# Rounding float64 weights on the chip: the last addition moved from VectorE to TensorE and to transfers

## The chip, the core and the metric

The kernel runs on one core of a Trainium2 chip. A core has five engines with a queue each: TensorE (PE, whose weight loads are shown as PEld), VectorE (DVE), ScalarE (ACT), GpSimd (POOL) and SyncE (SP). Each takes its instructions in the order in which they stand in its queue; an instruction that waits for another engine holds up all that stand behind it. Transfers (DMAs) are issued from the queues of SP, ACT and POOL and are done by 16 DMA engines. The metric is the time of one execution in microseconds on the device. Before the change it is 669.28 us, the median of three runs (668.96 to 669.71).

## The reference

Two blocks, one after the other: a gated linear attention over 768 steps for 4 batches of 8 heads with 48 channels, then a two-layer MLP with an ELU. The MLP's weights come in as float64.

```python
def _attn_ref(q, k, v, a_re, a_im):
    mag = np.sqrt(a_re * a_re + a_im * a_im)
    scale = np.minimum(mag, 0.999) / (mag + 1e-06)
    a_re_n, a_im_n = (a_re * scale, a_im * scale)
    for t in range(S):
        ar, ai = (a_re_n[:, :, t, :, None], a_im_n[:, :, t, :, None])
        new_re = ar * S_re - ai * S_im
        new_im = ar * S_im + ai * S_re
        kv = np.einsum('bhd,bhe->bhde', k[:, :, t], v[:, :, t])
        S_re, S_im = (new_re + kv, new_im)
        y[:, :, t] = np.einsum('bhd,bhde->bhe', q[:, :, t], S_re)

def _moe_ref(x, w_in, w_out):            # x: 3072 x 384, w_in: 384 x 2048, w_out: 2048 x 384
    h = x @ w_in
    g = np.where(h > 0.0, h, np.exp(np.minimum(h, 0.0)) - 1.0)
    return (g @ w_out).astype(np.float32)
```

## The kernel before

**Units.** The sequence is cut into chunks of 128 steps, and two batches go together: a unit `u` is one chunk of one pair of batches, 12 units in all (u = 0 and 1 are the first chunks of the two pairs). Each unit goes through the gates (`squares`, `joined`, `logarithms`, `powers`, `lengths`, `ratios`, `slopes`, `angles`, `decays`, `turns`, `waves`, `scaled`, `gated`), through the attention (`transposed`, `scores`, `states`, `values`, `seam`), and then through the MLP: eight pieces of `inner` (six matmuls of 128x256 against w_in, L1210) each with its `elu` (two ACT instructions, L1219 and L1220, and one on DVE, L1221, that reads the PSUM tile and so sets it free), and `project` (L1235 for the first units) against w_out. Later units (from u = 2 or 3) use forms of the two MLP products with fewer multiplications (`mult`, L1455; `product`, L1319), for which sums of the weights are made once (`summed_in`, `combined`).

**The weights.** Every weight comes as a pair of 32-bit words. A block is 128 partitions by 768 numbers; there are eight of w_in, `("in", m)`, and eight of w_out, `("out", m)`. `fetch` (L641) loads one as it is into a tile of raw words: into the tags g0 and g1 for the first four blocks of w_in, into one of two `w64` buffers for the others. `_rounded` (L36) makes from it two parts on DVE with four instructions: f from the high word (L40, L43), the power of two of f (L46), and p, the low word times that power (L50). A fifth, L655, adds p and f into the weight tile. f and p lie in the two buffers of the tag `wt`. `convert` issues one of these five instructions each time it is called, block after block.

**What sets the order.** The opening, up to the point where all weights are rounded and the first MLP is through, is a list written out by hand, `first`: each entry is a step, and its instructions go to the queues in the order of the list. Among the steps stand the `(convert,)` entries that thread the rounding through DVE's other work, `fetch` entries that put loads into SP's queue, and `(warm, n)`, n matmuls of the identity with itself whose result nobody reads (L1557). After the list follows a plan with due times, 16 slots to a unit, the same in both kernels.

**PSUM and buffers around the change.** `inner` takes its output from three buffers of the tag `mlp`; `outs()` gives two tiles y0 and y1 with one buffer each, which `values` and `project` use. w_out's tile is written for the first time when `("out", 0)` is rounded; before that nothing lies in it.

**Steps that the prediction names.** `joined` for u = 0 sums two tiles on PE by multiplying each with the identity (L720). `turned` (L832) does the sums of angles on PE (L837), takes them to turns on DVE (L842, L845), and for u = 0 and 1 makes the absolute value of the turns on DVE (L849). `angles` is ACT's arctan (L815), for which ACT loads a table. `ends` for u = 0 and 1 is 16 small matmuls (L946), a copy on DVE (`once`, L951), and one more matmul and copy. `state_sums` holds DVE's sums of the states (L1077, L1079, L1081), which wait for PE's state products (L1064).

Of the kernel before, what the change touches and what calls it, by code (L numbers as in the profile page):

```python
# [16 lines left out]
C = 128  # L17
# [14 lines left out]
WF = 2  # L32
# [473 lines left out]
def kernel(  # L506
# [110 lines left out]
    def weights_of(kind, m):  # L617

        if kind == "in":
            n = WF * DM // NI  # L620
            dst, cols = w_in[:, :, ts(m, n)], ts(m, 2 * n)
            tag = "g" + str(m // 2) if m < 4 else "w64"
            t = sb.tile([C, WF * DM, 2], U32, tag=tag, bufs=2, name="w64")
# [23 lines left out]
    def rounded(kind, m):  # L647

        w, dst = raw.pop((kind, m))
        f = sb.tile([C, WF * DM], U32, tag="wt", bufs=2, name="wf")  # L650
        p = sb.tile([C, WF * DM], U32, tag="wt", bufs=2, name="wp")
        yield from _rounded(nc, w, f, p)
        n = dst.shape[-1]
        f, p = (x.bitcast(FP32).rearrange("p (b n) -> p b n", n=n) for x in (f, p))
        nc.vector.tensor_tensor(out=dst, in0=p, in1=f, op=ALU.add)  # L655
        done.append((kind, m))
        yield True

# [173 lines left out]
    def turned(u, n):  # L832
# [13 lines left out]
        if u < 2:  # L846
            if n == 0:
                x["cs"] = new("cs", 1, [C, NB * H, 2, D])
            nc.vector.tensor_scalar(  # L849
                out=x["cs"][:, n * H : (n + 1) * H, 0].bitcast(U32),  # L850
                in0=x["z"][:, n].bitcast(U32), scalar1=0x7FFFFFFF, scalar2=None,
                op0=ALU.bitwise_and,
            )
# [108 lines left out]
    def waves(u, part=None):  # L962
# [5 lines left out]
        for n in range(0, NB, step):  # L968
# [6 lines left out]
            if u > 1:  # L975
# [602 lines left out]
    def gates_of(u, *at):  # L1578
# [8 lines left out]
        (joined, 0, 0), (squared, "ai", 1), (joined, 0, 1), (logarithms, 0, 0),  # L1587
        (logarithms, 0, 1), (fetch, "in", 1), (fetch, "in", 2), (ratios, 0, 0), (lengths, 0, 0),
        (warm, 2), (warm, 1), (lengths, 0, 1), (sums, 1), *2 * [(convert,)],
        (table, "exp_and_others"), (ratios, 0, 1), (powers, 0, 0), (powers, 0, 1), (warm, 2),  # L1590
        (sums, 0), (warm, 1), (angles, 0, 0), (angles, 0, 1), (summed, 0), (summed, 1),
        (decayed, 0, 0), (turned, 0, 0), (decayed, 0, 1), (turned, 0, 1), (waves, 0, 0),
        (waves, 0, 1), (begun, 1), (warm, 1), (scaled, 0, "q", 0), (ends, 0), (scaled, 0, "k", 0),
        (scaled, 0, "k", 1), (scaled, 0, "q", 1), (warm, 1), (gated, 0, 0), (warm, 1), (noted, 0),
        (table, "natural_log"), (warm, 2), (gated, 0, 1), (warm, 2), *3 * [(convert,)],
        (transposed, 0, "k", 0), (transposed, 0, "q", 1), (carry_on, 0), (transposed, 0, "q", 0),
        *4 * [(convert,)], (scores, 0, 0), (transposed, 0, "k", 1), (scores, 0, 1), (load_a, 1),
        (squares, 1), (joined, 1), (fetch, "in", 3), (logarithms, 1), (states, 0, 0),
        (values, 0, 0), (powers, 1), (convert,), (states, 0, 1), (lengths, 1), (load_qk, 1),
        (convert,), (ratios, 1), (values, 0, 1), (seam, 0), (warm, 2), (warm, 2), (decays, 1),  # L1600
        (load_a, 2), (warm, 1), (inner, 0, 0), *2 * [(convert,)], (noted, 1), (scaled, 1),
        (warm, 4), (convert,), (load_v, 1), (slopes, 1), (ends, 1), *3 * [(convert,)],
        (inner, 0, 2), (elu, 0, 0), (convert,), (fetch, "in", 4), (angles, 1), (turns, 1),
        (waves, 1), (gated, 1, 0), (inner, 0, 4), (gated, 1, 1), (transposed, 1, "q", 0),
        (transposed, 1, "k", 0), (convert,), (scores, 1, 0), (load_v, 2), (convert,),
        (fetch, "in", 5), *2 * [(convert,)], (transposed, 1, "k", 1), (states, 1, 0), (convert,),
# [161 lines left out]
```

## Time and profile before

| | us |
|---|---|
| median of three runs | 669.28 (668.96 to 669.71) |
| the profiled execution | 669.23 |
| its span, first to last instruction | 667.1 |
| PE busy in the span | 639.6 (96%) |
| DVE busy | 503.6 (75%) |
| ACT busy | 419.2 (63%) |
| POOL busy | 154.4 (23%) |
| rounding on DVE: 16 x L40, L43, L46, L50, L655 | 8.9 + 15.3 + 8.9 + 15.3 + 15.2 |
| granted TensorE clock, mean | 0.993 |

The profile is of one execution. Its parts: busy time of each engine; the span in 40 slices of 16.7 us with the busy share of each engine in tenths; groups of instructions by line, with their tile names as out<-in, count, busy time and mean; and on request the instructions of an engine in order of time, where a bracket shows how long the engine had been idle before and what ended that. A matmul in fp32 shows as two records. The ends of matmuls are modelled, so records that lie behind one another can overlap by a tenth or two of a microsecond. Tile names leave out the numbers of buffers; `ee`, `g` and `mlp` are the MLP's, `wf` and `wp` are f and p, `n`, `cs`, `qg`, `kg`, `S` belong to the gates and the attention.

### The profile page before, as it was taken

To read this page: it belongs to the slowest core of one execution; us is meant where nothing else is said; L and a number is where in the kernel's file an instruction comes from. 1 tells how busy PE (TensorE), PEld (TensorE's weight loads), DVE (VectorE), ACT (ScalarE), POOL (GpSimd) and SP (SyncE) were. 2 spreads that over 40 slices of the span, in tenths; PEclk is the share of its full clock that TensorE was granted. 3 is DMA by queue.
4 is the path that set the end of the run, shared out by engine and by line. 5 is a ranking of instruction groups with operands and counts; after the bars stand their busy time and mean duration, and the time that the engine had idled before them with its cause. 6 is when DMAs were issued, how large, how long until landed. Compare 5 with 4: busy or idle time off the path is not lost.

```text
span 667.1 us, 17231 instructions
## 1 busy us (share of the span) xinstructions
PE 639.6 (96%) x7236; PEld 579.6 (87%) x7236; DVE 503.6 (75%) x801; ACT 419.2 (63%) x684; POOL 154.4 (23%) x200
## 2 busy tenths in 40 slices
PE   8899899999999899999999999999999999999995
PEld 6777786576898798998998998999999999999995
DVE  5889999968777788678678768768768768765481
ACT  6885455874846567667677677677677577471250
POOL 2000000112124303503503503503603602402000
PEclk9799999999999999999999999999999999999999
DMA  9986645630900632452451451451551551212100
GB/s 166 189 142 105 148 149 167 112 72 20 154 3 15 115 56 62 81 106 57 86 106 53 90 104 48 97 104 44 100 104 44 102 104 43 54 32 61 34 2 29
DMA packets 151443, 56.12 MB, mean 84 GB/s; under 512 B 129684, under 2 KB 143164, under 8 KB 151356
## 3 DMA queue, kind: packets, MB, share of 16 engines
q1 hardware_dynamic: 147616, 53.58, 38.8%
q0 software_dynamic: 3520, 1.20, 1.5%
q8 instruction: 59, 0.97, 0.6%
q14 instruction: 28, 0.23, 0.1%
q10 hardware_dynamic: 220, 0.14, 0.1%
HBM read 48.91 MB, written 4.80 MB: 81 GB/s over the span
## 4 chain that ended last, share of the span: by engine, by line
PE 44%; DVE 10%; ACT 8%; issue 3%; DMA 1%; SPq 0%; ACTq 0%; DVEq 0%
PE mlp L1319 18%; PE mlp L1455 10%; PE y L1455 5%; DVE g L1471 3%; PE w L1023 3%; DVE g L1480 3%; PE y L1109 2%; ACT ee L1477 2%; ACT ee L1476 2%; PE w L1064 2%; PE w L837 2%; DVE g L1297 1%; ACT L735 1%; DVE n L772 1%; ACT n L746 1%
## 5 line engine op out<-in xcount | busy, mean ns | idle before, releaser
L1319 PE MATMUL mlp<-w_out,g 128*128 128x192 f32 x640 | 111.8, 328 | 1.0 <-DVE ee L1331 1.0
L1319 PEld LDWEIGHTS mlp<-w_out,g 128*128 128x128 f32 x640 | 104.2, 190 | 4.4 <-DVE ee L1331 1.6
L1081 POOL TENSOR_TENSOR S<-S,T 128x384 f32<-128x384 f32 x36 | 30.9, 857 | 175.5 <-DVE S L1079 175.5
L1210 PE MATMUL mlp<-x,w_in 128*128 128x256 f32 x288 | 65.1, 381 | 3.0 <-DVE g L1221 2.6
L1210 PEld LDWEIGHTS mlp<-x,w_in 128*128 128x128 f32 x288 | 53.8, 190 | 11.7 <-DVE g L1221 3.1
L1471 DVE TENSOR_TENSOR g<-g,mlp 128x512 f32<-128x512 f32 x45 | 30.7, 682 | 40.1 <-ACT qt L1024 28.7
L1297 DVE TENSOR_TENSOR g<-g 128x512 f32<-128x512 f32 x80 | 54.4, 695 | 5.0 <-PE mlp L1319 3.8
L1455 PE MATMUL mlp<-x,w_in 128*128 128x128 f32 x424 | 56.2, 275 | 0.4 <-DVE o L1344 0.4
L1480 DVE SCALAR_TENSOR_TENSOR g<-ee,g 128x512 f32<-128x512 f32 x63 | 47.6, 755 | 11.1 <-ACT ee L1477 11.0
L1319 PE MATMUL mlp<-w,g 128*128 128x192 f32 x320 | 54.5, 329 | 0.0
L1319 PEld LDWEIGHTS mlp<-w,g 128*128 128x128 f32 x320 | 51.8, 190 | 0.6
L1455 PEld LDWEIGHTS mlp<-x,w_in 128*128 128x128 f32 x424 | 51.6, 192 | 0.8 <-DVE o L1344 0.6
L1476 ACT ACTIVATE ee<-g 128x512 f32<-128x512 f32 x63 | 39.5, 627 | 17.2 <-DVE g L1471 16.7
L1190 POOL DMA_DIRECT2D x<-y x62 | 29.8, 488 | 87.2 <-ACT y L1126 37.3
L1468 ACT COPY g<-mlp 128x512 f32<-128x512 f32 x36 | 21.1, 586 | 44.0 <-PE mlp L1455 43.7
L1477 ACT ACTIVATE ee<-ee 128x512 f32<-128x512 f32 x72 | 45.4, 631 | 2.3
L1024 ACT COPY qt<-w 128x512 f32<-128x512 f32 x48 | 25.8, 589 | 15.5 <-PE w L1023 15.4
L973 ACT ACTIVATE cs<-n 128x768 f32<-128x768 f32 (+1 forms) x14 | 10.5, 751 | 38.0 <-DVE n L845 37.9
L904 ACT ACTIVATE n<-w 64x384 f32<-64x384 f32 (+1 forms) x60 | 28.1, 486 | 8.9 <-PE w L889 8.3
L1455 PE MATMUL mlp<-x,g 128*128 128x128 f32 x224 | 29.7, 275 | 1.2 <-DVE o L1344 1.2
L1219 ACT ACTIVATE ee<-mlp 128x512 f32<-128x512 f32 x24 | 14.3, 595 | 25.6 <-PE mlp L1210 17.2
L1455 PE MATMUL y<-x,w_in 128*128 128x128 f32 x216 | 29.0, 277 | 1.4 <-ACT g L1468 1.4
(222 smaller groups left out, 1434.8 us busy)
## 6 DMA issues: line engine op xcount, KB each, us to landing
w<-in_moe_w_out_dram SPq DMA_DIRECT2D x8, 768.0 KB
g<-in_moe_w_in_dram SPq DMA_DIRECT2D x24, 256.0 KB
g<-in_moe_w_out_dram SPq DMA_DIRECT2D x24, 256.0 KB
w<-in_moe_w_in_dram SPq DMA_DIRECT2D x16, 288.0 KB
vn<-in_v_dram SPq DMA_DIRECT2D x24, 192.0 KB
ar<-in_a_re_dram SPq DMA_DIRECT2D x22, 192.0 KB
ai<-in_a_im_dram SPq DMA_DIRECT2D x22, 192.0 KB
q<-in_q_dram SPq DMA_DIRECT2D x22, 192.0 KB
```

The source lines that it names most:

```text
L904: nc.scalar.activation(out=flat(x[key][to, n : n + 1]), in_=t[of], func=AF.Exp, scale=sign)
L1024: nc.scalar.copy(out=o[:, h0 : h0 + 4], in_=t)
L1081: eng.tensor_tensor(out=new_s, in0=new_s, in1=wide, op=ALU.mult)
L1190: eng.dma_start(out=x["x"][ds(j * HP + D, G), i], in_=x["y"][ds(j * HP + i * G, G)])
L1210: nc.tensor.matmul(t[:, e], lhsT=w_in[:, i, ts(f + e, C)], rhs=x["x"][:, i], start=(i == 0), stop=(i == NI - 1),)
L1297: nc.vector.tensor_tensor(out=S_of(u, k, h), in0=a, in1=b, op=op)
L1319: nc.tensor.matmul(to, lhsT=a[:, m], rhs=b[:, m], start=(first and h == 0 and m == 0), stop=False, skip_group_check=True,)
L1455: nc.tensor.matmul(x["c" + c][:, ts(m, C)], lhsT=a[:, m], rhs=x["mix"][p], start=(p == BANKS[c][0] and m == 0), stop=False, skip_group_che ...
L1471: nc.vector.tensor_tensor(out=part(u, to), in0=part(u, a), in1=part(u, b), op=op)
L1476: nc.scalar.activation(out=e, in_=part(u, of), func=AF.Relu, scale=-1.0)
L1477: nc.scalar.activation(out=e, in_=e, func=AF.Exp, scale=-1.0)
L1480: nc.vector.scalar_tensor_tensor(out=part(u, to), in0=nat[u]["e", to], scalar=-1.0, in1=part(u, of), op0=ALU.add, op1=ALU.max,)
```

## The change

Four things are changed.

1. `rounded` no longer ends with L655 for all blocks. For blocks 1 to 5 of w_in (`by_matmul`) f and p are left in a part of w_out's tile, and a new step `added(m)` multiplies both with the identity on PE, one after the other into the same PSUM tile (512 columns into y0, 256 into y1), from where two ACT copies bring the sums into w_in. For all blocks of w_out, f is made in w_out itself and p is added to it by a transfer from POOL's queue that accumulates. Blocks 0, 6 and 7 of w_in keep the addition on DVE.
2. The raw words of blocks 4 and 5 of w_in go into a part of w_out's tile too, not into `w64`.
3. The absolute value in `turned` for u = 1 moves to ACT, into `waves`.
4. The list `first` is new from `seam(0)` on: the `added` steps are put in, seven `warm` matmuls are left out, several `fetch`, `inner` and `elu` steps stand elsewhere, and there are fewer `convert` entries.

```diff
@@ weights_of
-            tag = "g" + str(m // 2) if m < 4 else "w64"
-            t = sb.tile([C, WF * DM, 2], U32, tag=tag, bufs=2, name="w64")
+            if m in (4, 5):
+                t = w_flat[:, ts(m - 4, 2 * WF * DM)].rearrange("p (n two) -> p n two", two=2)
+            else:
+                tag = "g" + str(m // 2) if m < 4 else "w64"
+                t = sb.tile([C, WF * DM, 2], U32, tag=tag, bufs=2, name="w64")
@@ rounded
-        f = sb.tile([C, WF * DM], U32, tag="wt", bufs=2, name="wf")
-        p = sb.tile([C, WF * DM], U32, tag="wt", bufs=2, name="wp")
-        yield from _rounded(nc, w, f, p)
-        n = dst.shape[-1]
-        f, p = (x.bitcast(FP32).rearrange("p (b n) -> p b n", n=n) for x in (f, p))
-        nc.vector.tensor_tensor(out=dst, in0=p, in1=f, op=ALU.add)
+        if kind == "out":
+            f = dst.bitcast(U32).rearrange("p f n -> p (f n)")
+            p = sb.tile([C, WF * DM], U32, tag="wt", bufs=2, name="wp")
+        elif by_matmul(m):
+            f, p = (w_flat[:, ts(4 + m % 2 * 2 + n, WF * DM)] for n in range(2))
+        else:
+            f = sb.tile([C, WF * DM], U32, tag="wt", bufs=2, name="wf")
+            p = sb.tile([C, WF * DM], U32, tag="wt", bufs=2, name="wp")
+        each = _rounded(nc, w, f, p)
+        for _ in range(3):
+            yield next(each)
+        next(each)
+        f, p = f.bitcast(FP32), p.bitcast(FP32)
+        if kind == "out":
+            nc.gpsimd.dma_start(
+                out=dst.rearrange("p f n -> p (f n)"), in_=p, accum_op=ALU.add
+            )
+        elif by_matmul(m):
+            parted[m] = f, p, dst
+            yield True
+            return
+        else:
+            yield True
+            f, p = (x.rearrange("p (b n) -> p b n", n=dst.shape[-1]) for x in (f, p))
+            nc.vector.tensor_tensor(out=dst, in0=p, in1=f, op=ALU.add)
         done.append((kind, m))
         yield True
+    w_flat = w_out.bitcast(U32).rearrange("p f n -> p (f n)")
+    def by_matmul(m):
+        return 0 < m < 6
+    def added(m):
+        f, p, dst = parted.pop(m)
+        n = dst.shape[-1]
+        for t, (i, k) in zip(outs(), ((0, 2), (2, 1))):
+            for x in (f, p):
+                nc.tensor.matmul(
+                    t[:, 0 : k * n], lhsT=ident, rhs=x[:, ds(i * n, k * n)], start=(x is f),
+                    stop=(x is p),
+                )
+            nc.scalar.copy(
+                out=dst[:, ds(i, k)], in_=t[:, 0 : k * n].rearrange("p (i n) -> p i n", n=n)
+            )
+        done.append(("in", m))
@@ turned
+        if u < 1:
             nc.vector.tensor_scalar(
                 out=x["cs"][:, n * H : (n + 1) * H, 0].bitcast(U32),
@@ waves
-            if u > 1:
+            if u > 0:
                 nc.scalar.activation(out=cos, in_=z, func=AF.Abs)
```

The list from `seam(0)` to the first projection, before:

```python
(seam, 0), (warm, 2), (warm, 2), (decays, 1), (load_a, 2), (warm, 1), (inner, 0, 0),
*2 * [(convert,)], (noted, 1), (scaled, 1), (warm, 4), (convert,), (load_v, 1), (slopes, 1),
(ends, 1), *3 * [(convert,)], (inner, 0, 2), (elu, 0, 0), (convert,), (fetch, "in", 4),
(angles, 1), (turns, 1), (waves, 1), (gated, 1, 0), (inner, 0, 4), (gated, 1, 1),
(transposed, 1, "q", 0), (transposed, 1, "k", 0), (convert,), (scores, 1, 0), (load_v, 2),
(convert,), (fetch, "in", 5), *2 * [(convert,)], (transposed, 1, "k", 1), (states, 1, 0),
(convert,), (inner, 0, 6), (fetch, "in", 6), (elu, 0, 2), *4 * [(convert,)],
(transposed, 1, "q", 1), (scores, 1, 1), (fetch, "in", 7), (values, 1, 0), (states, 1, 1),
(values, 1, 1), (convert,), (seam, 1), *4 * [(convert,)], (inner, 0, 8), (inner, 0, 10),
(elu, 0, 4), *2 * [(convert,)], (elu, 0, 6), (elu, 0, 8), (fetch, "out", 0), (warm, 2),
(inner, 1, 0), (convert,), (inner, 0, 12), (convert,), (inner, 1, 2), *3 * [(convert,)],
(inner, 1, 4), (fetch, "out", 1), (fetch, "out", 2), (fetch, "out", 3), (elu, 0, 10), (convert,),
(inner, 0, 14), (elu, 1, 0), *3 * [(convert,)], (elu, 0, 12), (fetch, "out", 4),
...
(project, 0, 0, 0, 4),
```

and after:

```python
(seam, 0), (fetch, "in", 4), (warm, 2), (warm, 2), (decays, 1), (added, 1), (inner, 0, 0),
*2 * [(convert,)], (noted, 1), (scaled, 1), (inner, 0, 2), (fetch, "in", 5), (convert,),
(load_v, 1), (slopes, 1), (ends, 1), (added, 2), (convert,), (elu, 0, 0), (angles, 1),
(turns, 1), (convert,), (waves, 1), (convert,), (load_a, 2), (fetch, "in", 6),
(inner, 0, 4), (gated, 1, 0), (added, 3), (gated, 1, 1), (transposed, 1, "q", 0),
(transposed, 1, "k", 0), (convert,), (elu, 0, 2), (scores, 1, 0), (inner, 0, 6),
(load_v, 2), (convert,), (fetch, "in", 7), (convert,), (transposed, 1, "k", 1),
(states, 1, 0), (convert,), (elu, 0, 4), (added, 4), (convert,), (transposed, 1, "q", 1),
(scores, 1, 1), (convert,), (inner, 0, 8), (values, 1, 0), (states, 1, 1), (convert,),
(elu, 0, 6), (values, 1, 1), (convert,), (seam, 1), (added, 5), *2 * [(convert,)],
(fetch, "out", 0), (inner, 0, 10), (elu, 0, 8), *2 * [(convert,)], (inner, 1, 0),
(convert,), (elu, 0, 10), (convert,), (inner, 0, 12), (convert,), (inner, 1, 2),
(elu, 1, 0), *2 * [(convert,)], (fetch, "out", 1), (fetch, "out", 2), (inner, 1, 4),
(elu, 0, 12), (convert,), (inner, 0, 14), (elu, 1, 2), (fetch, "out", 3), *3 * [(convert,)],
(fetch, "out", 4), *2 * [(convert,)], (inner, 1, 6), *2 * [(convert,)], (fetch, "out", 5),
...
(project, 0, 0, 0, 4),
```

A step that puts work on several engines puts it into each queue at its place in the list: `(added, 2)` stands ahead of `(elu, 0, 0)` and `(angles, 1)` on ACT as it stands ahead of `(turns, 1)` on PE. The order of the later steps of the list is the same but for the number of `convert` entries between them.

## The prediction

> **What bounds the kernel now.** I read first the busy tenths over 40 slices, then the busy time by stage, then the PE queue's order of time, and last the ACT queue at the place where the change cuts in. The first two rows show that after the opening only PE is full; in the opening DVE is full too.
>
> ```profile
> PE   8899899999999899999999999999999999999995
> ...
> DVE  5889999968777788678678768768768768765481
> ```
>
> By stage (columns: stage, its length, then busy us and count of PE, PEld, DVE, ACT, POOL, the granted clock, the DMA share and GB/s):
>
> ```profile
> 20.00:41.70 21.70, 19.09 (x279) 16.88 (x279) 19.69 (x29) 16.94 (x33) 0.97 (x2) 0.85 1.01 157
> 41.70:79.08 37.38, 32.56 (x443) 27.47 (x443) 34.69 (x52) 21.53 (x42) 1.92 (x4) 1.00 0.75 133
> 79.08:103.98 24.90, 23.48 (x111) 20.34 (x109) 24.35 (x35) 12.18 (x20) 0.00 (x0) 1.00 0.47 157
> 103.98:137.00 33.02, 32.94 (x171) 19.95 (x172) 31.28 (x39) 25.60 (x33) 2.38 (x3) 1.00 0.54 121
> 137.00:216.00 79.00, 78.49 (x911) 65.20 (x911) 56.30 (x79) 49.86 (x86) 20.54 (x26) 1.00 0.30 56
> ```
>
> DVE is 93 to 98% busy from 41.7 to 137 us and that is what the change takes from. But PE is 87% busy already from 41.7 to 79 and from 79 on it has almost no idle left. Whether that PE time is real work is the main question, because the ends of matmuls are modelled. The PE queue answers it:
>
> ```profile
> 47.79 2.86 PE L1210 MATMUL mlp<-x,w_in 128*128 128x256 f32 x12
> 50.48 1.45 PE L837 MATMUL w<-n,sum_turns 128*128 128x384 f32 x4
> ...
> 70.43 2.86 PE L1210 MATMUL mlp<-x,w_in 128*128 128x256 f32 x12
> 75.94 2.86 PE L1210 MATMUL mlp<-x,w_in 128*128 128x256 f32 x12 [2.65 <-DVE g L1221]
> 78.63 0.61 PE L1557 MATMUL mlp<-ident 128*128 128x128 f32 x4
> 79.08 23.48 PE L1210 MATMUL mlp<-x,w_in 128*128 128x256 f32 x108
> 103.98 2.85 PE L1235 MATMUL mlp<-w_out,g 128*128 128x384 f32 x8 [1.42 <-DVE g L1221]
> ```
>
> One `inner` (12 records) takes 2.69 us alone (47.79 to 50.48) and 23.48/9 = 2.61 us in the row of nine; three of them from 164.1 to 172 us, where DVE has idle time, take 7.93/3 = 2.64. So the row of nine runs at PE's own pace, and DVE's fullness beside it costs PE nothing but the two bracketed waits. The waits of PE between 41 and 109 us are 2.65, 1.42, 0.92, 0.37, 0.36, 0.32, 0.28 and 0.24: 6.6 us together. That is all that relief of DVE can give back up to 109 us.
>
> **The change part by part.** *Taken from DVE:* the final add (L655, mean 0.955 us) of five w_in blocks and eight w_out blocks, 13 x 0.955 = 12.4, and two `cs` masks of u = 1 (L849, 0.36 each), 0.7: 13.1 us off DVE. On the path this is worth at most the 6.6 us above.
>
> *Added to PE:* each `added(m)` sends f and p through the identity, 2 x (512 + 256) = 1536 columns in fp32. The trace has the same operation, identity times a 128x384 fp32 tile, at `joined`: four matmuls, so 1536 columns,
>
> ```profile
> 6.74 2.75 PE L720 MATMUL w<-n,ident 128*128 128x384 f32 x8
> ```
>
> and they take 2.59 us to the next instruction and 2.75 with its tail; 2.65 is taken. Five of them are 13.2 us, on an engine with 6.6 us of gaps to put them in. Seven `warm` matmuls go (0.25 each, four fill 38.67 to 39.66): -1.7. If the new order were perfect, PE would end later by 13.2 - 1.7 - 6.6 = 4.9 us. This is the floor: 669.3 + 4.9 = 674.2.
>
> *Added to ACT:* two copies for each `added`, about 0.59 (128x512, L1024) and 0.37 (between the 0.32 of a 128x192 and the 0.48 of a 128x384 copy): 4.8 us in all, and two `Abs` of 0.5 (as L973 at 128x384, 0.52). ACT is 58% busy from 41.7 to 79, so the sum is covered; what costs is where they stand. ACT's queue in the kernel before reads here:
>
> ```profile
> 44.80 0.60 ACT L1219 ACTIVATE ee<-mlp 128x512 f32<-128x512 f32 x1 [0.29 <-PE mlp L1210]
> 45.42 0.63 ACT L1220 ACTIVATE ee<-ee 128x512 f32<-128x512 f32 x1
> 46.07 1.28 ACT L815 ACT_TABLE_LOAD   x1
> 47.37 0.84 ACT L815 ACTIVATE n<-n 128x768 f32<-128x768 f32 x1
> ```
>
> *The new order, walked with these durations.* Nothing differs on PE up to 41.0 us. Then PE has `added(1)` to 43.65, `inner(0,0)` to 46.3, `inner(0,2)` to 48.9, the matmuls of `ends(1)` to 51.1 (2.2, as from 45.58 to 47.79 before), `added(2)` to 53.75, and then `turns(1)`, which needs ACT's arctan. ACT's queue now holds the copies of `added(2)` ahead of `elu(0,0)`, the table load and the arctan: 53.75 + 0.4 + 1.25 + 1.28 + 0.85 = 57.55. So PE stands 3.9 us with `inner(0,4)` behind the waiting matmul, DVE's `once` has stood from 46.5 to 50.5, and the chain of u = 1 (turns, waves, gated) is 7.2 us late. DVE then does turns, the end of block 3 (62.4) and `gated` (65.9). On PE: turns to 58.95, `inner(0,4)` to 61.6, `added(3)` to 64.2, transposes to 66.0, 0.5 for ACT's copies, scores to 67.7, `inner(0,6)` to 70.3, transposes and states to 72.3. `added(4)` needs p of block 4. On DVE this stands behind `elu(0,2)` (its exp after a table load: 69.5), the mask, and the state sums, which wait for PE's states at 72.3: 74.9. PE waits 1.75 and is done at 76.7. In the same manner p of block 5 stands behind the state sums of n = 1 and is ready at 87.6: `added(5)` runs to 89.4 with 1.45 of waiting, and after 0.4 for ACT's copy `inner(0,10)` ends at 92.4. Before, it ended at 78.6. With a tail of some 0.2 after each wait (70.43 to 73.29 is 2.86 for 2.62) that is 14 to 15 us late; 13.2 of it is the added matmuls, the removed gaps and the new ones (8.3) nearly cancel.
>
> *After that* come ten `inner` and one projection, 30.6 us before (78.63 to 109.25). DVE rounds w_out in the same stretch. A block is now 0.6 + 0.99 + 0.6 + 0.99 = 3.2 us plus the `elu` between, but its load is issued when the second last block is done. Before it had 6.1 us for that (88.2 to 94.3) and DVE never waited: a load takes 6.1 us or less. At 6.1, loads hold DVE up for 1 to 1.5 us a block, and the `elu` behind give PE waits of about 1.0, 0.5 and 2.0 us where it had 1.42 and two `warm` before (0.5): +1.6. At 4.5 us there is no such wait: -1.5. I take the middle, 0.
>
> *The accumulating transfers* (8, issued by POOL, 384 KB each) are in no row. POOL is idle from 73 to 130 us, an issue costs 0.5 to 0.95 (L1190, L957). Per block, p must be added before its buffer is written again two blocks on; the walk leaves 7.5 us. From below: a 16 KB POOL transfer lands in 1.7 us. From above: 384 KB read twice and written once is less than twice a w_out load of 768 KB, so with the load beside it 6.1 + 6.1 us, and about 13 with the issue. I take 6 to 7 (nearest to the large load), which is covered; projections need block m some 5 to 15 us after its add. At 13 the cover is gone and DVE comes late for `lengths(2)` and `turns(2)`.
>
> [...]
>
> *From 109 us on* the queues are as before and PE is full (78.49 of 79.00 to 216), so the delay is carried to the end. *Sum:* +14 to +15 at the end of the opening. The profiled execution took 669.23 (span 667.1 and 2.1 around it), the median is 669.28: 669.3 + 14.7 = 684.
>
> **The rivals.** *A, well packed, 675 to 678:* my chain of waits is too pessimistic, PE's new gaps are 0 to 4 us in place of 8.3. For it: single waits rest on sums of 0.1 us. Against: the arctan stands behind four ACT steps that cannot begin before `added(2)` ends. *B, the accumulating transfers bind, 688 to 695:* a two-block cycle of 13 + 1.55 us is 7.3 a block where the walk has 4.6; six blocks later DVE is 16 us late, less some 5 of cover. For it: DMA share is already 0.5 there and each block now moves twice the bytes. Decides from about 8 us a transfer. *C, the other side, 661:* the opening is DVE's. If what is shown as busy PE were waiting for DVE's buffers, the added matmuls would slip into it and the change would give the 6.6 us and 1.7 of `warm`: 669.3 - 8.3 = 661. It decides from 4.9 us of hidden waiting in PE's rows from 41 to 137. For it: DVE has no gap in that stretch. Against: 2.61, 2.64 and 2.69 us for an `inner` at any load of DVE. *D:* the 3.6 us of PE idle from 216 to 250 vanish as well; these waits (for `o`, and for a load queued behind the output) move along with PE, so D is only a part of A.
>
> **How the numbers follow.** The walk 0.62, A 0.20, B 0.14, C 0.04. A measurement here tells 0.2% (1.3 us) from no change. A, B and the walk all lie above +4.9, so faster 0.03, same 0.02 (parts of C and of A with D), slower 0.95. The range reaches from the floor of A to the middle of B: 675 to 692.
>
> **What would show it.** Right: L655's group falls from 16 to 3; five identity groups of about 2.7 us on PE; a PE wait of about 4 us for the arctan before the sums of angles of u = 1, and shorter ones at `added(4)` and `added(5)`, both for DVE; `inner(0,10)` ending near 92; DVE with idle time between 46 and 90. For B: DVE's L46 of the w_out blocks waiting for a DMA. Wrong: an `inner` clearly shorter than 2.6 us, the identity sums well under 2.6 us, or first projections before 110 us.

## The result, and the profile after

The changed kernel takes 692.98 us (median of four runs, 689.36 to 699.17) against 669.50 (four runs, 668.96 to 669.71): a ratio of 1.0362, 95% interval 1.0272 to 1.0452. It is slower, as forecast, but by 23.5 us where the forecast had 14.7, and the median is 1 us above the range (two of the four runs, 689.36 and 689.63, lie inside it). The profiled execution took 696.32 (span 694.6), so it is one of the longer ones.

Busy tenths of PE and DVE, the granted clock of PE and the DMA share, in 40 slices of 17.4 us, from the page of the changed kernel:

```profile
PE   8797899898999979999999999999999999999996
...
DVE  5764468785767787867858858858858858856481
...
PEclk9988999999999999999999999999999999999999
DMA  9979216893092053244343443451560560211100
```

DVE's row of nines (slices 4 to 8 before) is gone, but PE now has sevens in slices 2 and 4, its clock shows an 8 twice, and the DMA share is at 8 and 9 in slices 8 and 9, where it was at 6 and 3. By stage of the changed kernel (columns as in the prediction); the boundaries are the last `warm`, the end of inner(0,10), the first projection, and the first transposes of u = 2:

```profile
20.00:42.60 22.60, 18.17 (x270) 16.28 (x270) 16.59 (x25) 15.90 (x30) 0.09 (x1) 0.80 0.93 150
42.60:99.10 56.50, 48.67 (x479) 35.95 (x479) 30.11 (x46) 27.55 (x54) 2.80 (x6) 0.94 0.56 88
99.10:126.27 27.17, 24.34 (x110) 20.13 (x108) 23.49 (x33) 12.53 (x20) 3.00 (x4) 1.00 0.68 184
126.27:166.25 39.98, 36.48 (x176) 21.62 (x177) 29.35 (x37) 27.73 (x35) 8.90 (x10) 0.96 0.77 165
```

The first projection begins at 126.27 where it began at 103.98 (+22.3), the transposes of u = 2 at 166.25 where they began at 138.77 (+27.5). The span grew by the same 27.5 (667.1 to 694.6): nothing is lost or won behind 166 us. In the last row PE is busy for 36.5 of 40.0 us where it had no gap before, and the DMA share is 0.77 in it. The PE queue of the changed kernel shows the places (start, duration, line, operation; in brackets the idle time before it and what ended that):

```profile
35.29 0.65 PE L1153 MATMUL y<-qt,S 128*48 128x64 f32 x16 [2.47 <-DVE S L1121]
35.88 3.65 PE L1108 MATMUL mlp<-vn,kg 64*128 64x48 f32 x32
...
44.36 2.74 PE L693 MATMUL y<-w_out,ident 128*128 128x512 f32 x8
46.94 5.34 PE L1254 MATMUL mlp<-x,w_in 128*128 128x256 f32 x24
...
61.05 2.93 PE L880 MATMUL w<-n,sum_turns 128*128 128x384 f32 x4 [3.78 <-ACT n L858]
63.77 4.15 PE L1254 MATMUL mlp<-x,w_in 128*128 128x256 f32 x12
...
81.49 1.99 PE L693 MATMUL y<-w_out,ident 128*128 128x512 f32 x6 [1.64 <-DVE w_out L50]
...
94.67 1.99 PE L693 MATMUL y<-w_out,ident 128*128 128x512 f32 x6 [0.87 <-DVE w_out L50]
96.50 21.23 PE L1254 MATMUL mlp<-x,w_in 128*128 128x256 f32 x96
...
126.27 2.85 PE L1279 MATMUL mlp<-w_out,g 128*128 128x384 f32 x8 [2.06 <-DVE g L1265]
...
142.80 0.88 PE L933 MATMUL w<-n,sum_logs 64*64 64x384 f32 x8 [0.77 <-DVE n L815]
...
160.79 1.15 PE L1108 MATMUL w<-vn,kg 64*64 64x48 f32 x64 [2.73 <-DVE kg L1047]
161.87 4.54 PE L1279 MATMUL y<-w_out,g 128*128 128x384 f32 x8
```

Two things are to be seen. An `added` takes what was forecast (44.36 to 46.94, 2.58 us, with 2.65 taken), and the waits for the arctan (3.78, forecast 3.9), before `added(4)` (1.64, forecast 1.75) and before `added(5)` (0.53 and 0.87, forecast 1.45) are there. But the work *behind* three of the waits takes longer than its kind: the 32 state products at 35.88 take 3.65 us (1.99 in the kernel before), the `inner` at 63.77 4.15 (2.75), the four projection steps at 161.87 4.54 (2.85). The granted clock in these stretches is 0.66, 0.66 and 0.76:

```profile
34.00:44.00 10.00, 8.71 (x107) 7.92 (x108) 7.10 (x11) 6.02 (x14) 0.97 (x2) 0.66 0.66 102
58.00:68.00 10.00, 6.96 (x17) 4.99 (x18) 5.72 (x9) 7.21 (x11) 0.49 (x1) 0.66 1.05 152
...
160.00:167.00 7.00, 6.21 (x79) 4.08 (x80) 6.02 (x7) 5.33 (x9) 2.30 (x2) 0.76 0.49 96
```

The kernel before has one such fall, from 19.7 to 26.5 us, and then none until its last 3 us. The last wait, 2.73 us for kg, is followed back through the queues of ACT and DVE in the changed kernel:

```profile
152.53 0.84 ACT L752 ACTIVATE n<-ar 128x768 f32<-128x768 f32 x1 [1.86 <-DMA ar<-in_a_re_dram]
154.25 0.84 ACT L753 ACTIVATE n<-ai 128x768 f32<-128x768 f32 x1 [0.88 <-DMA ai<-in_a_im_dram]
...
155.13 0.96 DVE L759 TENSOR_TENSOR n<-n 128x768 f32<-128x768 f32 x1 [0.78 <-ACT n L753]
158.98 1.76 DVE L1047 TENSOR_TENSOR kg<-k,cs 128x1536 f32<-128x1536 f32 x1 [2.90 <-ACT cs L1021]
```

The loads of the decays of u = 3 land late; their squares stand on ACT's queue ahead of the sine and cosine that kg of u = 2 needs, and PE waits for kg. In the kernel before ACT begins the same squares at 127.73 us without a wait for a load. The loads of w_out are late as well:

```profile
133.24 0.56 DVE L40 TENSOR_SCALAR w_out<-w 128x768 uint32<-128x768 uint32 x1 [2.67 <-DMA w<-in_moe_w_out_dram]
...
135.46 0.56 DVE L46 TENSOR_SCALAR wp<-w_out 128x768 uint32<-128x768 uint32 x1 [0.64 <-DMA w_out<-wp]
```

DVE waited 5.8 us in four places for w_out's raw blocks, where it never waited before.

### The profile page after: what moved, and what is told of

Same layout as the page of the kernel before. It is cut to its first block, busy times and chain, and to the rows that moved or that the text cites. A ratio compares the mean times of both kernels' runs of the same rounds, so it can differ in the third digit from the quotient of the medians.

```text
span 694.6 us, 17297 instructions
## 1 busy us (share of the span) xinstructions
PE 657.4 (95%) x7262; PEld 587.9 (85%) x7262; DVE 490.9 (71%) x786; ACT 424.8 (61%) x696; POOL 161.6 (23%) x208
## 3 DMA queue, kind: packets, MB, share of 16 engines
q0 software_dynamic: 4672, 4.35, 4.0%
## 4 chain that ended last, share of the span: by engine, by line
PE 42%; DVE 9%; ACT 8%; issue 3%; DMA 1%; SPq 0%; ACTq 0%; DVEq 0%
PE mlp L1363 17%; PE mlp L1499 10%; PE y L1499 5%; DVE g L1515 3%; PE w L1067 3%; DVE g L1524 3%; PE y L1153 2%; ACT ee L1521 2%; ACT ee L1520 2%; PE w L1108 2%; PE w L880 2%; DVE g L1341 1%; ACT L778 1%; DVE n L815 1%; ACT n L789 1%
## 5 line engine op out<-in xcount | busy, mean ns | idle before, releaser
L1254 PE MATMUL mlp<-x,w_in 128*128 128x256 f32 x288 | 66.5, 387 | 0.8 <-DVE g L1265 0.8
L1515 DVE TENSOR_TENSOR g<-g,mlp 128x512 f32<-128x512 f32 x45 | 30.6, 681 | 40.2 <-ACT qt L1068 28.7
L1520 ACT ACTIVATE ee<-g 128x512 f32<-128x512 f32 x63 | 39.5, 627 | 17.4 <-DVE g L1515 17.0
L1108 PE MATMUL w<-vn,kg 64*64 64x48 f32 x1280 | 27.9, 221 | 3.6 <-DVE kg L1047 2.7
L1108 PEld LDWEIGHTS w<-vn,kg 64*64 64x64 f32 x1280 | 24.1, 134 | 8.3 <-DVE kg L1047 3.3
```

Source lines behind the costliest of these rows:

```text
L1108: nc.tensor.matmul(to, lhsT=of, rhs=vn[u % 2][ts(c, L), n, ts(h, D)], start=True, stop=True,)
L1254: nc.tensor.matmul(t[:, e], lhsT=w_in[:, i, ts(f + e, C)], rhs=x["x"][:, i], start=(i == 0), stop=(i == NI - 1),)
L1515: nc.vector.tensor_tensor(out=part(u, to), in0=part(u, a), in1=part(u, b), op=op)
L1520: nc.scalar.activation(out=e, in_=part(u, of), func=AF.Relu, scale=-1.0)
```

## Experiments

In each, the time of the kernel before was taken on the same chip in the same session (medians 671.06 us for `sums_on_dve`, `no_transfers`, `added2_later` and `wait_filled`; 671.58 for `list_only`, `transfers_only`, `elu_earlier` and `sums_on_pool`; 670.56 for the four kernels about what a wait costs; 670.37 for `five_transfers` and `after_five`); the ratio is against that.

### The change in parts

`sums_on_dve` keeps the new list, the raw blocks in w_out and the transfers, and puts DVE's addition back for the five blocks of w_in; `no_transfers` does the same for w_out alone; `list_only` does both, so that only the list, the raw blocks and the Abs remain; `transfers_only` is the kernel before with nothing but the accumulating transfers.

```diff
 sums_on_dve and list_only, in added(m):
-        for t, (i, k) in zip(outs(), ((0, 2), (2, 1))):
...
+        nc.vector.tensor_tensor(out=dst, in0=p, in1=f, op=ALU.add)
 no_transfers and list_only, in rounded("out", m):
-            nc.gpsimd.dma_start(
-                out=dst.rearrange("p f n -> p (f n)"), in_=p, accum_op=ALU.add
-            )
+            flat_dst = dst.rearrange("p f n -> p (f n)")
+            nc.vector.tensor_tensor(out=flat_dst, in0=p, in1=f, op=ALU.add)
 transfers_only, in the kernel before:
+        if kind == "out":
+            f = dst.bitcast(U32).rearrange("p f n -> p (f n)")
...
+            nc.gpsimd.dma_start(
+                out=dst.rearrange("p f n -> p (f n)"), in_=p.bitcast(FP32), accum_op=ALU.add
+            )
...
```

> The changed kernel with the five sums of w_in's blocks 1 to 5 done by one DVE addition each, at the same places of the list, in place of PE and ACT; accumulating transfers, raw blocks in w_out and the new list stay. Theory A (PE was full, so the five identity sums of 2.65 us and the waits that they bring on ACT's and DVE's queues are most of the loss): 13.2 us of PE work goes, the 3.8 us wait for the arctan and the 2.5 us of waits for p go, and with them the fall of the granted clock at 60 to 68 us (2.8); 23.5 us of loss shrink to 2 to 7: 671 to 677. Theory B (the accumulating transfers are the loss): most of it stays, 685 or more.

> The changed kernel with w_out's sums done by DVE in place (p added into f) in place of the accumulating transfers; the five PE sums and the new list stay. Theory A: PE's work and waits up to 99 us stay; what goes is DVE's waiting for w_out's loads (5.8 us after the change) against 7.6 us more work on DVE, so the later part moves by -4 to +2: 687 to 695. Theory B: 670 to 680. In the trace, A expects PE to reach the first projection within 2 us of the changed kernel's 126 us; the loads of w_out should again land in about 6 us or less if the transfers slowed them, and stay at 7.6 to 8.8 us late in the stage if it was the other loads.

> The changed kernel with both kinds of sums back on DVE: the five sums of w_in as one addition each at the places of the added steps, w_out's sums in place. What is left of the change is the new list, the raw blocks in w_out and the absolute value on ACT. Theory A2 (the new list, with its inner steps tied to sums that now come later in DVE's queue, costs by itself, and the transfers cost some 3 to 5 us after the first projection): the first projection starts at 110 to 115 us as in sums_on_dve (114), and from there to the state products of u = 2 it is 31 us as before, so the time is 676 to 681. Theory A (only the PE sums and transfers cost): the first projection starts by 106 us and the time is 669 to 673.

> The kernel before with one part of the change: f of w_out's blocks is made in w_out and p is added by an accumulating transfer from POOL's queue; list, w_in's sums and raw blocks as before. It takes 7.6 us off DVE between 84 and 128 us. If PE decides there (it is full from 79 us), nothing is won: 670 to 673. If the transfers slow the loads of w_out and DVE then comes late for gated(2), PE waits 2 to 4 us before the state products of u = 2, with or without a fall of the granted clock behind: 673 to 678. If DVE decided the stage, up to 7.6 us are won: 663 to 667.

| kernel | median us (range, runs) | ratio, 95% interval |
|---|---|---|
| list_only | 681.03 (679.69 to 682.18, 4) | 1.0153, 1.0128 to 1.0178 |
| sums_on_dve | 684.24 (679.21 to 687.52, 4) | 1.0169, 1.0106 to 1.0231 |
| no_transfers | 690.09 (688.22 to 695.04, 4) | 1.0301, 1.0253 to 1.0350 |
| transfers_only | 676.25 (671.07 to 679.03, 10) | 1.0074, 1.0052 to 1.0096 |
| the whole change | 692.98 (689.36 to 699.17, 4) | 1.0362, 1.0272 to 1.0452 |

Added in the order list, sums on PE, transfers, the steps are 1.53, 1.48 and 0.61%: 10.2, 9.9 and 4.1 us of 669.3. The last step lies within its two intervals; that the transfers cost is shown by `transfers_only`, 0.52 to 0.96%, 3.5 to 6.4 us. In this order each part costs and none gives back; beside DVE's additions the transfers make no difference that can be told (`sums_on_dve` 1.0169 against `list_only` 1.0153). `no_transfers` and `list_only` came out where their theories A and A2 had them, the second at the upper edge; what the raw blocks and the Abs cost apart from the list was not tried. `sums_on_dve` missed what was expected of it, since the new list alone already costs 10 us when DVE carries the additions. The list was written for a DVE with less to do: without the sums on PE, PE stands for DVE's sums, for the gates and for the elu, as its waits from 36 to 118 us in `list_only` show (engine, waiting group, what ended it: us in total, times, longest):

```profile
PE mlp L1246 <- DVE w_in L691: 5.1, 2, 3.5
PE w L1059 <- DVE qg L1039: 3.0, 1, 3.0
PE mlp L1271 <- DVE g L1257: 2.5, 1, 2.5
PE mlp L1246 <- DVE g L1257: 2.2, 2, 1.2
```

So the 9.9 us of the sums on PE can be read as 13.2 us of products less a part of these 12.8 us of waits, whose place they take. `no_transfers` lets the walk of the opening be read without a disturbance in its first 40 us: its inner(0,10) ends at 93.7 (the row of seven starts at 91.07), where the walk said 92.4. It begins `added(1)` at 40.16 and not at 41.0, so from there it is 2.1 us longer than the walk; 1.6 of these are `turns` and inner(0,4) at a slow clock (0.57 from 56 to 60 us) behind the wait for the arctan.

`transfers_only` fell into the range expected of it, 5 us slower with everything else as before. Its one long wait comes from the decays of u = 3. ACT's queue in `transfers_only`:

```profile
128.41 0.84 ACT L719 ACTIVATE n<-ar 128x768 f32<-128x768 f32 x1 [5.05 <-DMA ar<-in_a_re_dram]
132.53 0.84 ACT L720 ACTIVATE n<-ai 128x768 f32<-128x768 f32 x1 [3.28 <-DMA ai<-in_a_im_dram]
```

PE then stands 7.87 us for kg at 139.07, its only wait over 0.2 us from 95 to 145 us. The two waits of ACT (1.4 to 5.1 us for ar, 0.8 to 3.7 for ai), and 4.1 to 5.8 us of DVE waiting for w_out's raw blocks, are in all six profiles with the eight transfers, and in none of the eight without. SP's queue differs in the same stretch: its issues of k and ar for u = 3 take 6.90 and 3.58 us in `transfers_only` and 6.59 and 3.73 in the changed kernel, 3.58 and 0.99 in the kernel before.

### The wait for the arctan

`added2_later` puts added(2) behind turns(1), so that ACT's copies no longer stand ahead of the arctan; `wait_filled` leaves the order and fills PE's wait with 14 products of the identity that nothing reads.

```diff
 added2_later:
-        (ends, 1), (added, 2), (convert,), (elu, 0, 0), (angles, 1), (turns, 1), (convert,),
+        (ends, 1), (convert,), (elu, 0, 0), (angles, 1), (turns, 1), (added, 2), (convert,),
 wait_filled:
-        (ends, 1), (added, 2), (convert,),
+        (ends, 1), (added, 2), (filled, 14), (convert,),
```

> The changed kernel with one step moved: added(2) stands behind turns(1) in the list, not ahead of elu(0,0) and angles(1). Nothing else differs. If the wait for the arctan comes from the place of ACT's two copies, as the prediction had it, PE has no wait of over 1 us before the sums of angles of u = 1, no fall of the granted clock follows there, and the first projection starts 4 to 7 us earlier than in the changed kernel's profile: 684 to 689. If the wait has another cause, it stays at about 3.8 us and the time at 689 to 697.

> The changed kernel with 14 matmuls of the identity with itself (0.25 us each, results unread) put between added(2) and turns(1), where PE otherwise stands 3.8 us for the arctan. Theory C (a standstill of PE of 2.5 us or more brings the granted clock down for the next 7 to 8 us): the clock stays at 1.00 from 56 to 68 us, turns(1) and the next inner take 1.3 and 2.65 us, not 2.72 and 3.98, and 2 to 3 us are won although PE's work grows by 3.5: 686 to 691. Without C (the clock falls for reasons of its own): the clock falls there all the same, and the time is as before this edit or up to 1 us longer.

`added2_later` took 694.05 us (684.38 to 697.10, four runs; 1.0351, 1.0302 to 1.0400), `wait_filled` 695.23 (690.85 to 702.05; 1.0387, 1.0319 to 1.0456): by the times neither differs from the changed kernel. In the profiles the local effect is there. PE queue of `added2_later`:

```profile
51.35 1.56 PE L880 MATMUL w<-n,sum_turns 128*128 128x384 f32 x4
52.74 2.74 PE L693 MATMUL y<-w_out,ident 128*128 128x512 f32 x8
55.32 2.83 PE L1254 MATMUL mlp<-x,w_in 128*128 128x256 f32 x12
```

No wait, and an `inner` of 2.83 us behind it instead of 4.15. The first projection begins at 116.22 instead of 126.27 (6.6 us are from here, 3.4 from a load that came late in the changed kernel's profile, of which below), and this execution, 684.38 us, is the shortest of its kernel; the other three took 691.6 to 697.1. So the gain of 3.8 us of wait and 2.8 of slow matmuls is seen in one profile and is not established in the times, whose spread of 13 us hides it. Nor is the cause of that spread shown: one execution is profiled, and the others leave only a span and a mean clock (0.990 in the shortest, 0.977 in the longest). `wait_filled` missed: without the fall at 60 us a new one stood at 52 to 56 (the granted clock was 0.50 from 54 to 56), behind `ends(1)`, whose 16 products (32 records) have two columns each. Such a fall, of 3.4 us each time, stands behind `ends(1)` in `elu_earlier`, `stall_filled` and `no_late_warms`, and in no other profile.

### What a wait costs behind itself

`stall_bare` is the kernel before with one wait put into PE's queue where it otherwise runs without gaps: a product, ten ACT copies one after the other, and a product that reads the last copy. In `stall_filled` PE has nine products to do meanwhile. `no_late_warms` leaves out the seven `warm` products that the new list leaves out. `late_filled` is the changed kernel with nine products ahead of the place where PE stood for kg at 160 us.

```diff
 stall(n, fill), ahead of (inner, 1, 14): stall(9, 0) in stall_bare, stall(9, 9) in stall_filled:
+        nc.tensor.matmul(t, lhsT=ident, rhs=ident, start=True, stop=True)
+        nc.scalar.copy(out=o[:, 0:C], in_=t)
+        for _ in range(n):
+            nc.scalar.copy(out=o[:, 0:C], in_=o[:, 0:C])
...
+        for f in range(fill):
+            nc.tensor.matmul(t, lhsT=ident, rhs=w_out[:, f % 4], start=True, stop=True)
...
+        nc.tensor.matmul(t, lhsT=ident, rhs=o[:, 0:C], start=True, stop=True)
 no_late_warms:
-        (load_a, 2), (warm, 1), (inner, 0, 0),
+        (load_a, 2), (inner, 0, 0),
...
-        (warm, 4), (convert,), (load_v, 1),
+        (convert,), (load_v, 1),
...
-        (fetch, "out", 0), (warm, 2), (inner, 1, 0),
+        (fetch, "out", 0), (inner, 1, 0),
 late_filled:
-        (states, 2, 0),
+        (filled, 9), (states, 2, 0),
```

> The kernel before, with one wait put into PE's queue ahead of inner(1,14) (about 107 us, where PE runs at full clock and ACT stands idle): a 128-column product, ACT copies of it one after the other, and a product that reads the last copy; both products are read by nothing. From 0.27 us an ACT copy of this size PE should stand some 3.0 to 3.5 us. Theory 'a wait costs the clock behind it': the granted clock falls to about 0.5 for some 6 us from about 110 us, and the time is 6 to 7.5 us above the kernel before and 3 to 4 above the same kernel with the wait filled by products. Rival 'a wait costs its own length': +3 to +3.6, no fall of the clock, within 1 us of the filled one.

> The kernel before with the same wait put in, but PE runs nine products of the identity with 384 columns of w_out (0.34 us each, 3.1 together, read by nothing) while ACT copies. Both theories: the clock stays at 1.0 behind it and the time is 3 to 4 us above the kernel before. It is the measure for the kernel with the bare wait.

> The kernel before without the seven warm products that the new list leaves out (one ahead of inner(0,0), four ahead of ends(1), two ahead of inner(1,0)); nothing else. Theory 'they held the clock, and the new list lost it with them': a fall of the clock at 40 to 60 us or at 80, and the time 2 to 4 us above the kernel before. Rival 'they are idle filling of waits': no fall, the time within 1 us of the kernel before, or up to 1.5 us under it.

> The changed kernel with nine products of the identity with 384 columns of w_out (3.1 us of PE, read by nothing) ahead of the state products of u = 2, where PE stood 2.7 us for kg at 160 us and the clock then fell. Theory 'the late loss is that wait and the clock behind it': the fall at 162 to 165 is gone, the wait falls under 0.5, and the time is 0 to 3 us under the changed kernel's. Rival 'the clock there has another cause, or it isn't worth 3 us': the time is 0 to 3 us above it.

| kernel | median us (range, runs) | ratio, 95% interval |
|---|---|---|
| stall_bare | 676.53 (674.66 to 681.81, 6) | 1.0105, 1.0068 to 1.0143 |
| stall_filled | 678.76 (675.62 to 680.62, 5) | 1.0117, 1.0085 to 1.0149 |
| no_late_warms | 672.19 (669.48 to 675.09, 11) | 1.0027, 1.0007 to 1.0047 |
| late_filled | 696.77 (694.83 to 699.20, 5) | 1.0383, 1.0356 to 1.0409 |

The fill was mis-sized: here a product of 384 columns shows as two records of 0.33 us, so nine take 6.0 us and not 3.1. So the two times can't be set against each other, but the two PE queues can. `stall_bare`:

```profile
111.26 0.75 PE L1572 MATMUL mlp<-o,ident 128*128 128x128 f32 x2 [3.32 <-ACT o L1567]
111.80 4.22 PE L1210 MATMUL mlp<-x,w_in 128*128 128x256 f32 x12
115.85 5.32 PE L1235 MATMUL y<-w_out,g 128*128 128x384 f32 x16
```

and `stall_filled`:

```profile
116.32 0.38 PE L1572 MATMUL mlp<-o,ident 128*128 128x128 f32 x2
116.54 2.86 PE L1210 MATMUL mlp<-x,w_in 128*128 128x256 f32 x12
119.23 5.32 PE L1235 MATMUL y<-w_out,g 128*128 128x384 f32 x16
```

Behind 3.3 us of standing the same `inner` takes 4.05 us to the next row, behind products 2.69. The granted clock is 0.57 from 111 to 115 us in the first kernel and 1.00 behind the fill in the second:

```profile
111.00:115.00 4.00, 3.74 (x11) 3.10 (x12) 1.91 (x3) 0.21 (x1) 0.00 (x0) 0.57 0.50 188
```

From the first projection to the end of inner(1,14) is 10.98 us here and 5.27 in the kernel before: 5.7 more, of which 3.3 is the wait, some 0.5 the two products, and 1.9 the slow clock. So in this pair of profiles the fall of the clock comes with the wait and not with the fill, at half the size that was expected (3 to 4 us): it lasts 3.4 us, not 6. Not every wait does this: 2.98 us in `list_only`, at 57.29, has no fall behind it. The last section shows what the falls go with. From there to the end the three kernels need 557.9, 557.6 and 557.6 us: a delay at 115 us goes to the end unchanged.

`no_late_warms` does less on PE (1.7 us) and is 0.07 to 0.47% slower: by this interval the `warm` products are worth a little more than they cost, which neither expectation had. In its profile the waits stand elsewhere, and the clock falls at 48 and at 106 us; `elu_earlier`, which keeps the `warm` products, has falls at the same two places (49.6 and 107.6), so these are not shown to come from leaving them out. In `late_filled` the wait for kg and the fall behind it are gone, as expected, and the six us of products bring the time, 3.8 us above the changed kernel's and so outside both ranges, to 1.0383 where the change has 1.0362, a difference inside the intervals; if the wait (2.73) and its fall (1.7) had cost nothing, it would be 6 us.

### The transfers beside the loads

`five_transfers` is `transfers_only` with DVE's addition back for blocks 5 to 7 of w_out, whose transfers run beside the loads of the decays; `after_five` is the changed kernel with the same edit.

```diff
-        if kind == "out":
+        if kind == "out" and m < 5:
 after_five, in both places of rounded, also:
-        elif by_matmul(m):
+        elif kind == "in" and by_matmul(m):
```

> The kernel before with accumulating transfers for w_out's blocks 0 to 4 alone; blocks 5 to 7 keep DVE's addition. With all eight (transfers_only) the loads of the decays of u = 3 landed late: ACT stood 5.05 us for ar and 3.28 for ai, DVE's kg of u = 2 came late and PE stood 7.87 us at 139 us. Theory 'the last three transfers, which run beside those loads, make them late': ACT's waits for ar and ai fall under 1 us in all, PE's wait for kg under 1, and the time is 669 to 673, at or just under the kernel before. Rival 'it is the loads' own queue, which the transfers of blocks 0 to 4 have already put back': ACT's waits stay above 4 us and the time stays at 674 to 678.

> The changed kernel with the same edit: blocks 5 to 7 of w_out summed by DVE again. Theory: ACT's waits for ar and ai (1.86 and 0.88 us) and PE's waits for DVE's n and kg behind them (0.77 and 2.73) go, with the fall of the clock at 162 to 165; from the first projection to the state products of u = 2 some 31 us instead of 34.5; the time 687 to 690 (693.0 less 3 to 6). Rival 'the late loads are not worth more than DVE's three additions, 2.9 us': 691 to 695.

`five_transfers` took 676.32 us (673.27 to 682.97, 12 runs; 1.0079, 1.0047 to 1.0111), `after_five` 695.44 (691.85 to 696.00, six runs; 1.0357, 1.0325 to 1.0389): no faster. The step that was in doubt came out as the theory said: in neither kernel does ACT wait for ar or ai of u = 3. The time missed (676.32 lies in the rival's range), and a new wait took the place of the old. Block 5's f lies in the pair of `wt` buffers again, and there the transfers of the blocks before it still read. DVE in `after_five`:

```profile
131.57 0.56 DVE L40 TENSOR_SCALAR wf<-w 128x768 uint32<-128x768 uint32 x1 [4.87 <-DMA w_out<-wp]
...
134.75 0.56 DVE L46 TENSOR_SCALAR wp<-wf 128x768 uint32<-128x768 uint32 x1 [1.60 <-DMA w_out<-wp]
```

PE still waits 0.78 us for n and 1.73 for kg there. In `five_transfers` DVE waits 3.96 us for a transfer at L46 of that block, and PE stands 5.5 us at 124.80. A version with three `wt` buffers was not tried.

### Two other orders of the kernel before

The forecast of the other side was that relief of DVE can gain the waits it causes. Two edits try that without PE or transfers: `elu_earlier` puts the elu that PE's longest wait (2.65 us) is for ahead of values(1,0); `sums_on_pool` gives all 16 additions to POOL, which is idle there.

```diff
 elu_earlier:
-        (fetch, "in", 7), (values, 1, 0), ... (inner, 0, 10), (elu, 0, 4),
+        (fetch, "in", 7), (elu, 0, 4), (values, 1, 0), ... (inner, 0, 10),
 sums_on_pool:
-        nc.vector.tensor_tensor(out=dst, in0=p, in1=f, op=ALU.add)
+        nc.gpsimd.tensor_tensor(out=dst, in0=p, in1=f, op=ALU.add)
```

> The kernel before with elu(0,4) moved ahead of values(1,0) in the list, so that ACT does it before its copies and the 2.7 us of issuing seam(1)'s transfers. In the profile of before PE waits 2.65 us for this elu before inner(0,10), the longest wait of the stage. If PE's waits are what can be won in the opening, this wins 1.5 to 2.7 us: 668.4 to 669.6 against 671.1. If the wait only moves to the next elu, the time stays within 0.7 us.

> The kernel before with the last addition of all 16 blocks on POOL in place of DVE; list as before. It takes 15.2 us off DVE and nothing is put on PE; an addition on POOL of 128x768 takes 1.9 us in the profile. If relief of DVE was worth having, as the change supposes, PE's waits of 6.6 us between 41 and 109 us shrink and 2 to 5 us are won: 666 to 669. If PE decides, at most 1.4 us (its wait before the first projection) is won: 669.5 to 671.5. If POOL's longer sums come too late for inner, or slow DVE beside them, it is slower: 672 to 676.

`elu_earlier` took 672.79 us (670.50 to 675.23, 12 runs; 1.0015, 0.9996 to 1.0033): no change. The wait of 2.65 became 0.9 and two of 0.3, and the wait ahead of the first projection grew from 1.42 to 2.3. `sums_on_pool` took 679.12 (678.75 to 680.00, four runs; 1.0123, 1.0101 to 1.0145): slower, with PE waiting 3.7 and 2.9 us for DVE's g. No version of this study is faster than the kernel before.

## Why the prediction was off

Right were the direction, and the mechanism as far as inner(0,10). *DVE* lost 12.7 us of busy time (503.6 to 490.9; 13.1 forecast) and PE's time did not shrink for it: rival C, in which `inner` hid DVE's waits, is out. *PE's sums* took 2.58 us each (2.65). *The walk* gave its waits within 0.2 us each, and `no_transfers` reaches the end of inner(0,10) at 93.7 us for 92.4. *Rival A* is out: no added wait was missing.

Off was the size, in three terms, all above the forecast. The profiled execution of the changed kernel is late by 27.5 us; the walk accounts for 13.8 of it (92.4 less 78.6). The rest:

1. *Durations at full clock.* Every step was priced as the kernel before runs it at clock 1.00, and a wait at its own length. Behind the wait for the arctan, `turns` and inner(0,4) took 2.72 and 3.98 us to their next rows where they take 1.29 and 2.61 before: 2.8 us. With the same wait of 3.78 us the two are 1.5 to 1.7 us over in `no_transfers`, `late_filled` and `after_five`, so part of the 2.8 is of this execution. Behind the wait for kg the projection took 4.38 for 2.68: 1.7. `stall_bare` against `stall_filled` shows such a fall behind a wait that is put in alone. A third fall, at 36 to 43 us, and a wait of 2.5 us ahead of it belong to a load of the decays of u = 1 that landed 2.1 us late in this execution: added(1) began at 44.36 instead of 41.0, 3.4 us. `added2_later` and `no_transfers`, of the same order up to there, don't have it; `late_filled` and `sums_on_dve` do, and so do `elu_earlier` and `stall_bare` with the old order, where ACT waits 1.74 and 1.23 us for the same load. So it is of the run and not of the change, and the median (3.3 us under the profiled execution) may well be without it; that was not shown.

2. *"After that ... I take the middle, 0".* From the end of inner(0,10) to the end of inner(1,14) it took 32.45 us instead of 30.6: +1.8. The upper end that the prediction named, +1.6 with loads of 6.1 us, fits it: DVE waited 1.40 and 0.44 us for w_out's blocks in this stretch.

3. *"The accumulating transfers ... which is covered", and "From 109 us on the queues are as before".* The transfer itself was sized right (median 7.1 us from issue to landing; 6 to 7 taken), and DVE waited only 0.64 us for one. Missed was what it does to the loads beside it. Rival B let the transfers bind by their own buffers; the price was paid by w_out's blocks, behind which DVE came late for u = 2 (PE waited 0.77 us), and by ar and ai (2.73): 3.5 us where PE had no gap. What the profiles show is that the waits for loads come with the transfers: they are in the six with all eight and in none of the eight without; by what the loads are held up is in no row here. Nor is it shown that a transfer reads 384 KB twice or that a block moves "twice the bytes", as the prediction and rival B reckoned: the page of the changed kernel counts 384 KB a transfer, beside 768 KB for a load of w_out (POOL's queue q0 carries 4.35 MB where it had 1.20).

13.8 + 3.4 + 2.8 + 1.8 + 3.5 + 1.7 is 27.0; the 0.5 left is spread over the opening. So the forecast lacked 4.5 us of slow clock behind two waits, 1.8 behind inner(0,10) and 3.5 beside the transfers. Without the load of this one run the profiled execution is late by 24.1, against 23.5 between the medians. The floor of the forecast, +4.9, was never near: the list's order had to be paid as well as the products.

## What to carry to other kernels

A wait on a full PE is priced with what it does to the matmuls behind it: here 3.3 us of standing cost 5.2, where the clock fell behind it. An addition that is moved from an engine to a transfer is not free because nothing waits for that transfer; look at which loads move beside it and who waits for the last of them (here ACT 1.86 and 0.88 us for ar and ai, and PE 2.73 us for kg behind them). And where an order written by hand is tight, a part of a change tried alone can cost what it does not cost within the whole (the list alone has 12.8 us of waits, whose place the sums on PE then take), so its price is read from steps that are added one after the other.

## What the runs showed that was not expected

The granted clock of PE falls in pieces of one length. By the clock records of the 16 traces there are 32 falls to 0.50 between 30 us and the last 4 us of a span: 23 last 3.41 us, eight 6.83 and one 10.24. Within a profile their starts lie whole multiples of 3.413 us apart, and where this grid begins differs from execution to execution. In these profiles the falls go with how long PE stands within one piece of the grid. The wait ahead of inner(0,10) is 2.65 us in the kernel before and 2.67 in `stall_bare`, which has the same order up to there; these are the pieces around it (columns as in the prediction), first of the kernel before, then of `stall_bare`:

```profile
70.90:74.31 3.41, 2.39 (x12) 1.75 (x10) 3.27 (x5) 0.60 (x3) 1.44 (x3) 1.00 0.44 111
74.31:77.73 3.42, 1.79 (x8) 1.61 (x9) 2.91 (x5) 3.05 (x6) 0.00 (x0) 1.00 0.96 163
77.73:81.14 3.41, 3.41 (x19) 3.05 (x19) 3.31 (x6) 1.23 (x2) 0.00 (x0) 1.00 0.76 232
...
73.79:77.21 3.42, 1.28 (x6) 1.15 (x7) 2.90 (x4) 3.21 (x6) 0.00 (x0) 1.00 1.00 197
77.21:80.62 3.41, 3.41 (x11) 2.79 (x10) 3.34 (x6) 0.61 (x2) 0.00 (x0) 0.50 0.76 191
```

In the kernel before the wait is split, 1.02 and 1.63 us, and the clock stays at 1.00; in `stall_bare` 2.14 us of it lie in one piece, and the next runs at 0.50. Over the 16 profiles, from 30 to 640 us, 22 pieces at full clock have PE standing for more than 1.96 us, and each has a fall behind it; of 15 with 1.60 to 1.96 us five have one. Below that there are five falls, four of them behind the two-column products of `ends(1)` with 0.27 to 0.73 us of standing in the piece; what thin products count for was not tried. A piece at 0.50 costs a full PE some 1.7 us (an estimate: half of 3.41).

The length of a wait alone does not decide it: those of 2.47 and 2.73 us in the changed kernel and of 1.99 in `late_filled` (before the first projection) had the clock at 0.50 behind them; those of 2.65 us in the kernel before and of 2.98 in `list_only` did not.

A second thing is the spread. The kernel before kept within 0.1% in its first four runs and within 0.9% in the later sessions; the changed one spreads over 1.4% and `added2_later` over 1.8%, with the mean clock lower in the longer runs (0.989 at 689.4 us, 0.979 at 699.2). The clock that is missing, 1 less the mean clock, times the span is 7.6 us in the first of these runs and 14.6 in the second, an estimate that would make 7 of the 9.8 us between them. Whether the place of the grid in each run is behind this was not shown, since one execution of a kernel is profiled.
